# Sixteen-point stages of a 2-D spectral filter: sixteen bursts of one row, or eleven of three rows

## The chip, the cores and the metric

The kernel runs on one core of a Trainium2 chip. The metric is device time in microseconds of one execution. The engines are TensorE (PE, with its weight loads as PEld), VectorE (DVE), ScalarE (ACT), GpSimd (POOL) and SyncE (SP), which here issues the DMAs.

## The reference

```python
x = A_x                       # (1, 2048, 640), bf16
xn = layernorm(x)
X = rfft2(xn over (2048, 640))
s = irfft2(X * (w_r + 1j * w_i))          # 2048 x 321 complex filter
g = silu((gelu(xn @ w_gate) * (xn @ w_up)) @ w_down)   # 640 -> 1536 -> 640
return x + s * g
```

So there are two branches from the same normalised input: a spectral filter (a two-dimensional real transform, a product with a complex filter, the inverse transform) and a gated FFN. They meet in one product and one sum.

## The kernel before, in words

The 2048 rows are split as 16 x 128. The forward transform goes in three stages: a 128-point stage per slab (`slab_S1`), the transform along the 640 columns (`pair_D`), which gives 321 frequencies, and a stage of sixteen points across the slabs. The last needs the data in another order, so `pair_D` stores its result to a scratch array in device memory (`ZDR`) and `load_B2` brings it back as `B2`, 128 partitions by 32 rows by 321 frequencies. The inverse goes the same way back: a sixteen-point stage, a scratch array `UDR`, `load_V`, a 128-point stage (`slab_S1i`) and the inverse along the columns (`pair_Di`).

The change touches the sixteen-point stages. Before, there are sixteen bursts, one for each h from 0 to 15. `pair_S2(h)` makes four matmuls of 64 x 64 weights (the four quadrants of the array) over the 321 frequencies of rows h and 16+h of `B2` into a pair of PSUM banks `px`. ScalarE copies `px` to `xs` (642 elements a partition), VectorE multiplies it with the filter's real part (`W1`) and imaginary part (`W2`), giving two products. `pair_S2i(h)` makes eight more matmuls of the two products into another pair of banks `pu`, the first four from the first product, the last four from the second. ScalarE copies `pu` out in two instructions, even and odd frequencies, into `us`, and SyncE stores `us` to `UDR` in two DMAs. Row 0 needs a matrix of its own in one of the quadrants (`kind`). The two PSUM pairs come from one pool of two.

The order on every engine is written out by hand. A list `back` has 144 steps: pieces of the FFN, which are either a half (`ffn_half`: five matmuls of 512 columns) or a third of the down projection (`down_third`: eight matmuls of 320 columns). `plan` says what of the spectral branch is put behind each step. `load_B2` stands behind step 54. The bursts stand behind steps 64 to 88: `pair_S2(h)` behind step 64 + 3h//2, and `pair_S2i(h-1)` right after it; the last `pair_S2i` and `load_V` stand behind step 88. So two bursts are one or two steps apart by turns. Steps 60 to 71 and 96 to 107 are down projections, 72 to 95 FFN halves. The first slab of the inverse 128-point stage stands behind step 96, and the gather that prepares it (`gather`, L579) behind step 95.

The filter rows come in 32 DMAs over SyncE (`w_rows`), and GpSimd halves the first and the last frequency (`w_edge`). The normalised input `X` (16 slabs of 640) is last read as a matmul or fold operand ahead of step 54; its slabs 12 to 15 are still read by transposing DMAs (`slab_T`) placed behind steps 65, 68, 71 and 74.

Of the kernel before, what the change touches and what calls it, by code (L numbers as in the profile page):

```python
# [10 lines left out]
BF16 = mybir.dt.bfloat16  # L11
INT32 = mybir.dt.int32
ACT = mybir.ActivationFunctionType
ALU = mybir.AluOpType
P = 128
S = 2048
D = 640
L = 321
LP = 322
LH = 161  # L20
# [3 lines left out]
NS = 16  # L24
NH = 32
# [5 lines left out]
@with_exitstack  # L31
def kernel(
    ctx: ExitStack,
    tc: tile.TileContext,
    A_x: bass.AP,
    A_w_r: bass.AP,
    A_w_i: bass.AP,
    B_x: bass.AP,
    B_w_gate: bass.AP,
    B_w_up: bass.AP,  # L40
    B_w_down: bass.AP,
    out: bass.AP,
):

    nc = tc.nc
    x2 = A_x[0]
    xv = x2.rearrange("(n2 n1) d -> n2 n1 d", n1=NS)
    outv = out[0].rearrange("(n2 n1) d -> n1 n2 d", n1=NS)  # L50

    consts = ctx.enter_context(tc.tile_pool(name="consts", bufs=1))
    big = ctx.enter_context(tc.tile_pool(name="big", bufs=1))
    wts = ctx.enter_context(tc.tile_pool(name="wts", bufs=1))
    xg = ctx.enter_context(tc.tile_pool(name="xg", bufs=5))
    work = ctx.enter_context(tc.tile_pool(name="work", bufs=2))
    psA = ctx.enter_context(tc.tile_pool(name="psA", bufs=2, space=bass.MemoryType.PSUM))
    psB = ctx.enter_context(tc.tile_pool(name="psB", bufs=2, space=bass.MemoryType.PSUM))
    dram = ctx.enter_context(tc.tile_pool(name="dscratch", bufs=1, space=bass.MemoryType.DRAM))

    ZDR = dram.tile([2, NS, P, L], BF16)
    UDR = dram.tile([2, NS, P, L], BF16)


    X = big.tile([P, NS, D], BF16, tag="sX")
    Wg = wts.tile([P, 5, F], BF16)
    Wu = wts.tile([P, 5, F], BF16)
    Wd = wts.tile([P, NT, D], BF16)
    W1 = wts.tile([P, NS, 2, L], BF16)
    W2 = wts.tile([P, NS, 2, L], BF16)  # L70
    wgv = B_w_gate.rearrange("(c p) f -> p c f", p=P)
    wuv = B_w_up.rearrange("(c p) f -> p c f", p=P)
    with tc.manual_schedule():
        build(nc, locals())


def build(nc, env):
    consts, big, wts, xg, work, psA, psB = (env[k] for k in ("consts", "big", "wts", "xg", "work", "psA", "psB"))
    ZDR, UDR, X, Wg, Wu, Wd, W1, W2 = (env[k] for k in ("ZDR", "UDR", "X", "Wg", "Wu", "Wd", "W1", "W2"))
    xv, outv, wgv, wuv = (env[k] for k in ("xv", "outv", "wgv", "wuv"))  # L80
# [28 lines left out]

    spw = [(WT, src.rearrange("(k1 r) l -> k1 r l", k1=NS)) for WT, src in ((W1, A_w_r), (W2, A_w_i))]  # L110

    def w_rows(i, hh, ri, pm):
        WT, sp = spw[i]
        p0 = hh * 64 + ri * 2 + pm
        for lo in range(2):
            u0 = lo * 32 + hh * 16
            if pm == 0:
                nc.sync.dma_start(out=WT[p0:p0 + 61:4, :, lo, :], in_=sp[:, u0:u0 + 16, :])
            elif u0 == 0:
                nc.sync.dma_start(out=WT[p0:p0 + 61:4, 1:NS, lo, :], in_=sp[:, 127:112:-1, :])  # L120
                nc.sync.dma_start(out=WT[p0:p0 + 61:4, 0, lo, :], in_=sp[:, 64, :])
            else:
                nc.sync.dma_start(out=WT[p0:p0 + 61:4, :, lo, :], in_=sp[:, 128 - u0:112 - u0:-1, :])

    def w_edge(i):
        WT = spw[i][0]
# [7 lines left out]
    MG = consts.tile([P, 2, 2, 64], BF16)  # L134
    N1 = consts.tile([P, 2, P], BF16)
    N2 = consts.tile([P, 2, P], BF16)
# [29 lines left out]
    xf = {}  # L166
# [347 lines left out]
    st_b = {}  # L514

    def load_B2():
        B2 = big.tile([P, NH, L], BF16, tag="sB", name="B2")
        zv = ZDR.rearrange("c n (z a k h) l -> a (c n z) k h l", z=2, a=2, k=2)
        B4 = B2.rearrange("p (k h) l -> p k h l", k=2)
        for h0, h1 in ((0, 1), (1, 4), (4, 8), (8, 12), (12, 16)):  # L520
            for lo in range(2):
                nc.sync.dma_start(out=B4[64 * lo:64 * lo + 64, :, h0:h1, :], in_=zv[lo][:, :, h0:h1, :])
        st_b["B2"] = B2

    def pair_S2(h):
        B2 = st_b["B2"]
        px = psB.tile([P, 2, 512], FP32, tag="b")
        for lo in range(2):
            r = slice(64 * lo, 64 * lo + 64)
            for hh in range(2):  # L530
                kind = 0 if h == 0 and lo == 0 and hh == 0 else 1
                nc.tensor.matmul(px[64 * hh:64 * hh + 64, lo, 0:L], lhsT=MG[r, kind, 0, :], rhs=B2[r, 16 * hh + h, :],  # L532
                                 start=True, stop=True)
        xs = work.tile([P, 2 * L], BF16, tag="m1", bufs=2)
        nc.scalar.copy(out=xs.rearrange("p (k l) -> p k l", k=2), in_=px[:, :, 0:L])  # L535
        p1 = work.tile([P, 2 * L], BF16, tag="p1", bufs=2)
        p2 = work.tile([P, 2 * L], BF16, tag="p2", bufs=2)
        for pp, WT in ((p1, W1), (p2, W2)):
            nc.vector.tensor_tensor(out=pp, in0=xs, in1=WT[:, h].rearrange("p k l -> p (k l)"), op=ALU.mult)  # L539
        st_b[h] = (p1, p2)  # L540

    uv = UDR.rearrange("c n (z a h) l -> a (c n z) h l", z=2, a=2)

    def pair_S2i(h):
        p1, p2 = st_b.pop(h)
        pu = psB.tile([P, 2, 512], FP32, tag="b")
        for NM, pp, first in ((N1, p1, True), (N2, p2, False)):
            for hh in range(2):
                r = slice(64 * hh, 64 * hh + 64)
                for lo in range(2):  # L550
                    kind = 0 if h == 0 and lo == 0 and hh == 0 else 1
                    nc.tensor.matmul(pu[64 * lo:64 * lo + 64, hh, 0:L], lhsT=NM[r, kind, 0:64],  # L552
                                     rhs=pp[r, lo * L:(lo + 1) * L], start=first, stop=not first)
        us = work.tile([P, 2, L], BF16, tag=("xf", "uv")[h % 2], bufs=2, name="us")
        nc.scalar.copy(out=us[:, :, 0:LH], in_=pu[:, :, 0:L:2])
        nc.scalar.copy(out=us[:, :, LH:L], in_=pu[:, :, 1:L:2])
        for lo in range(2):
            nc.sync.dma_start(out=uv[lo][:, h:NH:16, :], in_=us[64 * lo:64 * lo + 64, :, :])

    st_c = {}  # L560

# [189 lines left out]
    def put(s, *item):  # L751
        plan[s].append(item)
# [57 lines left out]
    for pair in range(8):  # L810
        a = F0 + 3 * pair
# [3 lines left out]
        if pair < 6:  # L815
            b = a if pair < 4 else a + 3
# [6 lines left out]
    for k in range(16):  # L823
        put(8 + k if k < 8 else (32, 35, 38, 41, 44, 44, 47, 47)[k - 8], w_rows, k // 8, k % 8 // 4, k % 2, k % 4 // 2)
    put(40, w_edge, 0)
    put(z_end + 4, w_edge, 1)
    put(z_end, load_B2)
    put(z_end + 3, mg_turn)
    sb = z_end + 10
    for h in range(NS):  # L830
        put(sb + 3 * h // 2, pair_S2, h)
        if h > 0:
            put(sb + 3 * h // 2, pair_S2i, h - 1)
    sb += 24
    put(sb, pair_S2i, NS - 1)
    put(sb, load_V)
    vs0 = sb + 8
    for i, at in enumerate((vs0 - 1, vs0, vs0 + 6, vs0 + 16, vs0 + 25)):
# [2 lines left out]
    for pair in range(8):  # L841
        a = vs0 + 11 * pair // 2
# [55 lines left out]
```

## Time and profile before

| | |
|---|---|
| median of three runs | 207.86 us (207.09 to 207.91) |
| the profiled execution | 207.12 us |
| its span, first to last instruction | 205.3 us |
| granted TensorE clock, mean | 0.997 |
| TensorE busy | 198.7 us |
| ScalarE, VectorE, GpSimd busy | 124.7, 129.9, 33.9 us |

How to read it: a row of a timeline has the start, the length, the engine, the line of the kernel, the operation, what it writes and reads, the shape and how many instructions were merged; in brackets, how long the engine had been idle and whom it waited for. A matmul's length includes a modelled tail, so the distance between starts tells more. A row of a group (by line and shape) has the total busy time and the mean length of one in ns, then the idle time before them. A DMA row has the number of DMAs, the size of one, and the median time from issue to landing.

### The profile page before, as it was taken

The numbers are of one execution on the slowest core, as the hardware profiler recorded it, in microseconds if no ns is written. First come the engines' busy times: TensorE is split into PE (matmuls) and PEld (weight loads), VectorE is DVE, ScalarE is ACT, GpSimd is POOL, SyncE is SP. The second block draws the span as 40 slices with busy tenths as digits, with TensorE's granted clock in tenths as the row PEclk, the third lists the DMA queues.
The fourth block names the chain that finished last, engine by engine and source line by source line (L and its number), as shares of the span: only waits on it lengthen the run. The fifth ranks groups of instructions, "written<-read, shape, count | busy, mean of one in ns | idle before, by whom it ended". The sixth has DMA issues, their size and how long they took to land.

```text
span 205.3 us, 4412 instructions
## 1 busy us (share of the span) xinstructions
PE 198.7 (97%) x1626; PEld 121.2 (59%) x1643; DVE 129.9 (63%) x357; ACT 124.7 (61%) x230; POOL 33.9 (17%) x61
## 2 busy tenths in 40 slices
PE   7999999999999999999999999999999999999993
PEld 5788855777555555475644444447775555556762
DVE  7886966797678842336565655433568768775653
ACT  2547567767868787225787777424555654656641
POOL 5328688945001100000000000000000000000000
PEclk9999999999999999999999999999999999999998
DMA  5999999899987799289965332369731332242111
GB/s 168 303 305 314 369 291 135 168 146 179 176 161 169 166 186 172 68 198 229 192 137 108 73 67 65 82 139 294 228 86 74 96 123 74 63 132 78 66 51 65
DMA packets 46199, 31.81 MB, mean 155 GB/s; under 512 B 12512, under 2 KB 43872, under 8 KB 46176
## 3 DMA queue, kind: packets, MB, share of 16 engines
q1 hardware_dynamic: 46176, 31.52, 67.1%
q8 instruction: 13, 0.21, 0.5%
q14 instruction: 10, 0.08, 0.1%
HBM read 21.66 MB, written 7.88 MB: 144 GB/s over the span
## 4 chain that ended last, share of the span: by engine, by line
PE 90%; DVE 4%; DMA 2%; issue 1%; ACT 1%; POOL 1%; SPq 0%; DVEq 0%
PE psu L670 24%; PE psg L670 24%; PE psg L694 13%; PE psu L694 12%; PE pd L490 5%; PE pu L552 3%; PE pv L597 2%; PE pz L481 2%; DMA X<-in_A_x_dram 2%; PE pd L494 2%; PE px L532 2%; DVE st L174 1%; DVE uT L676 1%; POOL rst L190 1%; PE pt L326 0%
## 5 line engine op out<-in xcount | busy, mean ns | idle before, releaser
L670 PE MATMUL psu<-xnT,Wu 128*128 128x512 bf16 (+2 forms) x289 | 60.4, 339 | 0.6 <-issue 0.3
L670 PE MATMUL psg<-xnT,Wg 128*128 128x512 bf16 (+2 forms) x284 | 59.9, 338 | 0.8 <-issue 0.3
L676 DVE TENSOR_TENSOR uT<-psu,ge 128x512 bf16<-128x512 f32 (+2 forms) x59 | 34.4, 586 | 33.7 <-PE psu L670 27.4
L674 ACT ACTIVATE ge<-psg 128x512 bf16<-128x512 f32 (+2 forms) x59 | 30.6, 518 | 28.9 <-PE psg L670 27.6
L694 PEld LDWEIGHTS <-uT 128*128 128x128 bf16 x384 | 36.1, 98 | 15.2 <-issue 0.5
L670 PEld LDWEIGHTS <-Wu 128*128 128x128 bf16 x295 | 26.5, 98 | 21.8 <-issue 1.3
L670 PEld LDWEIGHTS <-Wg 128*128 128x128 bf16 x295 | 26.2, 98 | 20.9 <-issue 1.0
L694 PE MATMUL psg<-Wd,uT 128*128 128x320 bf16 (+1 forms) x192 | 30.4, 303 | 0.0
L694 PE MATMUL psu<-Wd,uT 128*128 128x320 bf16 (+1 forms) x192 | 29.6, 296 | 0.0
L539 DVE TENSOR_TENSOR p<-xs,W 128x642 bf16<-128x642 bf16 x32 | 14.4, 492 | 8.9 <-ACT xs L535 8.5
L502 ACT CAST zd<-pd 128x644 bf16<-128x644 f32 x15 | 12.3, 883 | 4.6 <-PE pd L494 4.6
L611 ACT ACTIVATE eo<-pd 128x640 bf16<-128x640 f32 x16 | 10.4, 701 | 7.4 <-PE pd L494 7.4
L599 ACT CAST vs<-pv 128x640 bf16<-128x640 f32 x16 | 11.0, 690 | 6.1 <-PE pv L597 6.1
L174 DVE BATCH_NORM_STATS2 st<-X 128x6 f32<-128x320 bf16 x32 | 14.1, 481 | 0.3 <-issue 0.2
L535 ACT CAST xs<-px 128x642 bf16<-128x642 f32 x16 | 11.1, 692 | 4.0 <-PE px L532 3.6
L620 DVE TENSOR_TENSOR cs<-eo 128x640 bf16<-128x640 bf16 x16 | 7.1, 485 | 7.5 <-ACT eo L611 7.5
L483 ACT CAST Z<-pz 128x640 bf16<-128x640 f32 x16 | 11.0, 694 | 1.1 <-PE pz L481 1.1
L190 POOL TENSOR_TENSOR rst<-ve,mhalf 128x1 f32<-128x1 f32 (+2 forms) x9 | 6.5, 719 | 27.2 <-DVE ve L188 27.2
L645 DVE TENSOR_TENSOR Yall<-Yall,G 128x640 bf16<-128x640 bf16 (+3 forms) x18 | 8.1, 450 | 1.8 <-ACT G L699 1.6
L703 DVE SCALAR_TENSOR_TENSOR G<-th,psg 128x320 bf16<-128x320 f32 x8 | 3.9, 486 | 7.6 <-ACT th L702 7.6
L646 DVE TENSOR_TENSOR Yall<-Yall,xt 128x640 bf16<-128x640 bf16 (+3 forms) x18 | 8.2, 454 | 0.6
L552 PE MATMUL pu<-p,N 64*64 64x321 bf16 x128 | 8.2, 304 | 0.1
(138 smaller groups left out, 213.1 us busy)
## 6 DMA issues: line engine op xcount, KB each, us to landing
ZDR<-zd SPq DMA_DIRECT2D x16, 160.5 KB, 4.2
UDR<-us SPq DMA_DIRECT2D x32, 80.2 KB, 2.6
xt<-in_A_x_dram SPq DMA_DIRECT2D x8, 320.0 KB, 3.2
W<-in_A_w_r_dram SPq DMA_DIRECT2D x14, 160.5 KB, 6.8
W<-in_A_w_i_dram SPq DMA_DIRECT2D x14, 160.5 KB, 5.1
out_dram<-Yall SPq DMA_DIRECT2D x14, 160.0 KB, 1.8
B<-ZDR SPq DMA_DIRECT2D x6, 321.0 KB, 8.4
Vin<-UDR SPq DMA_DIRECT2D x6, 321.0 KB, 5.8
```

What stands on the lines that cost most here:

```text
L174: nc.vector.bn_stats(out=st[:, k, :], in_=X[:, n1, 320 * k:320 * k + 320])
L483: nc.scalar.copy(out=Zt[n1], in_=pz)
L502: ev(out=zd.rearrange("p a c (m b) -> p a c m b", b=2)[:, :, :, :, b], in_=pd[b])
L535: nc.scalar.copy(out=xs.rearrange("p (k l) -> p k l", k=2), in_=px[:, :, 0:L])
L539: nc.vector.tensor_tensor(out=pp, in0=xs, in1=WT[:, h].rearrange("p k l -> p (k l)"), op=ALU.mult)
L552: nc.tensor.matmul(pu[64 * lo:64 * lo + 64, hh, 0:L], lhsT=NM[r, kind, 0:64], rhs=pp[r, lo * L:(lo + 1) * L], start=first, stop=not first)
L599: nc.scalar.copy(out=vs, in_=pv)
L611: nc.scalar.activation(out=eo[:, b], in_=py[b], func=ACT.Copy, scale=(2.0 if n0 // 4 in BY_SILU else 1.0) / (S * D))
L670: nc.tensor.matmul(ps, lhsT=WT[:, c, t * P:(t + 1) * P], rhs=xnT[g][:, c, c0:c1_], start=(c == 0), stop=(c == 4))
L674: nc.scalar.activation(out=ges[t], in_=ps, func=ACT.Gelu_apprx_tanh)
L676: nc.vector.tensor_tensor(out=uT[g][:, t, c0:c1_], in0=ps, in1=ges[t], op=ALU.mult)
L694: nc.tensor.matmul(ph, lhsT=uT[g][:, t, j * P:(j + 1) * P], rhs=Wd[:, t, c0:c1_], start=(t == 0), stop=(t == NT - 1))
```

## The change

A burst is now three rows h by about half of the frequencies: 162 or 159, so 486 or 477 columns of a PSUM bank. Rows 0 to 14 make ten such bursts, row 15 alone an eleventh of 321 columns. The matmuls, the copy to `xs`, the two products and the copies to `us` work on three rows at once. The frequencies of a row are split over two bursts, and both write into one `us` of three whole rows, which is stored in two DMAs once the second half is there. In the first two bursts, the quadrant that treats row 0 apart has two matmuls in place of one.

The filter tiles are laid out with rows of 322 elements and the two halves (`lo`) outside of the rows. The products and `us` no longer have tiles of their own: they lie in the first 13 slabs of `X`, two sets of each by turns. `load_B2` brings rows 0 to 2, 3 to 5, 6 to 8, 9 to 11 and 12 to 15, where it was 0, 1 to 3, 4 to 7, 8 to 11 and 12 to 15. Burst b stands behind step 64 + 24b//11, its second half behind the next burst's first, and the last second half behind step 87. `load_V` stays behind step 88.

```diff
-    W1 = wts.tile([P, NS, 2, L], BF16)
-    W2 = wts.tile([P, NS, 2, L], BF16)
+    W1 = wts.tile([P, 2, NS, LP], BF16)
+    W2 = wts.tile([P, 2, NS, LP], BF16)
...
-        for h0, h1 in ((0, 1), (1, 4), (4, 8), (8, 12), (12, 16)):
+        for h0, h1 in ((0, 3), (3, 6), (6, 9), (9, 12), (12, 16)):
...
+        sc = X[:, 0:13, :].rearrange("p n d -> p (n d)")
+        n_u, n_p = 2 * 3 * L, 2 * 3 * WB
+        st_b["p"] = sc[:, 0:4 * n_p].rearrange("p (s q k x) -> p s q k x", s=2, q=2, k=2)
+        st_b["u"] = sc[:, 4 * n_p:4 * n_p + 2 * n_u].rearrange("p (s k x) -> p s k x", s=2, k=2)
+
+    WB = LH + 1
+    BURSTS = [(h0, 3, l0, w) for h0 in range(0, 15, 3) for l0, w in ((0, WB), (WB, L - WB))]
+    BURSTS.append((15, 1, 0, L))
+
+    def s2_tiles(b, lo, hh):
+        h0, n = BURSTS[b][:2]
+        if h0 == 0 and lo == 0 and hh == 0:
+            return ((0, 1, 0), (1, n, 1))
+        return ((0, n, 1),)
...
-                kind = 0 if h == 0 and lo == 0 and hh == 0 else 1
-                nc.tensor.matmul(px[64 * hh:64 * hh + 64, lo, 0:L], lhsT=MG[r, kind, 0, :], rhs=B2[r, 16 * hh + h, :],
-                                 start=True, stop=True)
+                for i, j, kind in s2_tiles(b, lo, hh):
+                    ps = px[64 * hh:64 * hh + 64, lo, i * w:j * w].rearrange("p (h l) -> p h l", l=w)
+                    nc.tensor.matmul(ps, lhsT=MG[r, kind, 0, :],
+                                     rhs=B2[r, 16 * hh + h0 + i:16 * hh + h0 + j, l0:l0 + w], start=(i == 0),
+                                     stop=(j == n))
+
+        def wide(t):
+            return t[:, :, 0:n * (WB if n > 1 else LP)].rearrange("p k (h l) -> p k h l", h=n)[:, :, :, 0:w]
+
+        xs = wide(work.tile([P, 2, 3 * WB], BF16, tag="m1", bufs=2, name="xs"))
+        nc.scalar.copy(out=xs, in_=px[:, :, 0:n * w].rearrange("p k (h l) -> p k h l", l=w))
+        pp = []
+        for q, WT in enumerate((W1, W2)):
+            pp.append(wide(st_b["p"][:, b % 2, q]))
+            nc.vector.tensor_tensor(out=pp[-1], in0=xs, in1=WT[:, :, h0:h0 + n, l0:l0 + w], op=ALU.mult)
...
-        nc.scalar.copy(out=us[:, :, 0:LH], in_=pu[:, :, 0:L:2])
-        nc.scalar.copy(out=us[:, :, LH:L], in_=pu[:, :, 1:L:2])
-        for lo in range(2):
-            nc.sync.dma_start(out=uv[lo][:, h:NH:16, :], in_=us[64 * lo:64 * lo + 64, :, :])
+        us = st_b["u"][:, h0 // 3 % 2, :, 0:n * L].rearrange("p k (h l) -> p k h l", l=L)
+        pv = pu[:, :, 0:n * w].rearrange("p k (h l) -> p k h l", l=w)
+        for m in range(2):
+            c0 = m * LH + l0 // 2
+            nc.scalar.copy(out=us[:, :, :, c0:c0 + (w + 1 - m) // 2], in_=pv[:, :, :, m:w:2])
+        if l0 + w == L:
+            for lo in range(2):
+                nc.sync.dma_start(out=uv[lo][:, :, h0:h0 + n, :], in_=us[64 * lo:64 * lo + 64, :, :, :])
...
-    for h in range(NS):
-        put(sb + 3 * h // 2, pair_S2, h)
-        if h > 0:
-            put(sb + 3 * h // 2, pair_S2i, h - 1)
+    for b in range(len(BURSTS)):
+        put(sb + 24 * b // 11, s2_in, b)
+        if b > 0:
+            put(sb + 24 * b // 11, s2_out, b - 1)
+    put(sb + 23, s2_out, len(BURSTS) - 1)
     sb += 24
-    put(sb, pair_S2i, NS - 1)
     put(sb, load_V)
```

More of the change, by code (lines that the diff above doesn't have):

```diff
@@ L117, in w_rows @@
             if pm == 0:
-                nc.sync.dma_start(out=WT[p0:p0 + 61:4, :, lo, :], in_=sp[:, u0:u0 + 16, :])
+                nc.sync.dma_start(out=WT[p0:p0 + 61:4, lo, :, 0:L], in_=sp[:, u0:u0 + 16, :])
             elif u0 == 0:
-                nc.sync.dma_start(out=WT[p0:p0 + 61:4, 1:NS, lo, :], in_=sp[:, 127:112:-1, :])
-                nc.sync.dma_start(out=WT[p0:p0 + 61:4, 0, lo, :], in_=sp[:, 64, :])
+                nc.sync.dma_start(out=WT[p0:p0 + 61:4, lo, 1:NS, 0:L], in_=sp[:, 127:112:-1, :])
+                nc.sync.dma_start(out=WT[p0:p0 + 61:4, lo, 0, 0:L], in_=sp[:, 64, :])
             else:
-                nc.sync.dma_start(out=WT[p0:p0 + 61:4, :, lo, :], in_=sp[:, 128 - u0:112 - u0:-1, :])
+                nc.sync.dma_start(out=WT[p0:p0 + 61:4, lo, :, 0:L], in_=sp[:, 128 - u0:112 - u0:-1, :])
     def w_edge(i):
@@ L523, in load_B2, with s2_in @@
         st_b["B2"] = B2
-    def pair_S2(h):
+        sc = X[:, 0:13, :].rearrange("p n d -> p (n d)")
[10 more added lines that the diff above has]
+        return ((0, n, 1),)
+    def s2_in(b):
         B2 = st_b["B2"]
+        h0, n, l0, w = BURSTS[b]
         px = psB.tile([P, 2, 512], FP32, tag="b")
@@ L530, in pair_S2, with s2_out @@
             for hh in range(2):
-                kind = 0 if h == 0 and lo == 0 and hh == 0 else 1
-                nc.tensor.matmul(px[64 * hh:64 * hh + 64, lo, 0:L], lhsT=MG[r, kind, 0, :], rhs=B2[r, 16 * hh + h, :],
-                                 start=True, stop=True)
[L534 to L545, printed above, removed]
+                for i, j, kind in s2_tiles(b, lo, hh):
[11 more added lines that the diff above has]
+            nc.vector.tensor_tensor(out=pp[-1], in0=xs, in1=WT[:, :, h0:h0 + n, l0:l0 + w], op=ALU.mult)
+        st_b[b] = pp
+    uv = UDR.rearrange("c n (z a k h) l -> a (c n z) k h l", z=2, a=2, k=2)
+    def s2_out(b):
+        h0, n, l0, w = BURSTS[b]
+        pp = st_b.pop(b)
         pu = psB.tile([P, 2, 512], FP32, tag="b")
-        for NM, pp, first in ((N1, p1, True), (N2, p2, False)):
+        for q, NM in enumerate((N1, N2)):
             for hh in range(2):
@@ L550, in pair_S2i @@
                 for lo in range(2):
[L551 to L554, printed above, removed]
-        nc.scalar.copy(out=us[:, :, 0:LH], in_=pu[:, :, 0:L:2])
-        nc.scalar.copy(out=us[:, :, LH:L], in_=pu[:, :, 1:L:2])
-        for lo in range(2):
-            nc.sync.dma_start(out=uv[lo][:, h:NH:16, :], in_=us[64 * lo:64 * lo + 64, :, :])
+                    for i, j, kind in s2_tiles(b, lo, hh):
+                        ps = pu[64 * lo:64 * lo + 64, hh, i * w:j * w].rearrange("p (h l) -> p h l", l=w)
+                        nc.tensor.matmul(ps, lhsT=NM[r, kind, 0:64], rhs=pp[q][r, lo, i:j, :],
+                                         start=(q == 0 and i == 0), stop=(q == 1 and j == n))
+        us = st_b["u"][:, h0 // 3 % 2, :, 0:n * L].rearrange("p k (h l) -> p k h l", l=L)
[6 more added lines that the diff above has]
+                nc.sync.dma_start(out=uv[lo][:, :, h0:h0 + n, :], in_=us[64 * lo:64 * lo + 64, :, :, :])
     st_c = {}
```

## The prediction

> **What bounds the kernel now.** I read the page first: TensorE is busy for 97% of the span at full clock, and the chain that ended last is 90% TensorE.
>
> ```profile
> span 205.3 us, 4412 instructions
> PE 198.7 (97%) x1626; PEld 121.2 (59%) x1643; DVE 129.9 (63%) x357; ACT 124.7 (61%) x230; POOL 33.9 (17%) x61
> PEclk9999999999999999999999999999999999999998
> PE 90%; DVE 4%; DMA 2%; issue 1%; ACT 1%; POOL 1%; SPq 0%; DVEq 0%
> ```
>
> So an edit is worth what it takes from TensorE's own sequence, and nothing else, unless it makes TensorE wait. A busy figure hides small losses between matmuls, so I next read TensorE's timeline through the edited stage, 92 to 131 us, in order of starts.
>
> ```profile
> 91.86 0.71 PE L694 MATMUL psu<-Wd,uT 128*128 128x320 bf16 x4
> 92.50 0.33 PE L532 MATMUL px<-B,MG 64*64 64x321 bf16 x4
> 92.77 1.26 PE L694 MATMUL psu<-Wd,uT 128*128 128x320 bf16 x8
> ...
> 96.47 0.71 PE L694 MATMUL psu<-Wd,uT 128*128 128x320 bf16 x4
> 97.10 0.33 PE L532 MATMUL px<-B,MG 64*64 64x321 bf16 x4
> 97.26 0.45 PE L552 MATMUL pu<-p,N 64*64 64x321 bf16 x8
> 97.64 1.26 PE L694 MATMUL psu<-Wd,uT 128*128 128x320 bf16 x8
> ...
> 120.98 1.25 PE L670 MATMUL psu<-xnT,Wu 128*128 128x512 bf16 x5
> 122.16 0.33 PE L532 MATMUL px<-B,MG 64*64 64x321 bf16 x4
> 122.44 0.60 PE L552 MATMUL pu<-p,N 64*64 64x321 bf16 x8
> 122.98 1.25 PE L670 MATMUL psg<-xnT,Wg 128*128 128x512 bf16 x5
> ...
> 128.70 1.24 PE L670 MATMUL psg<-xnT,Wg 128*128 128x512 bf16 x5
> 129.87 0.47 PE L552 MATMUL pu<-p,N 64*64 64x321 bf16 x8
> 130.27 1.25 PE L670 MATMUL psu<-xnT,Wu 128*128 128x512 bf16 x5
> 131.36 1.24 PE L670 MATMUL psg<-xnT,Wg 128*128 128x512 bf16 x5
> 139.75 1.79 PE L694 MATMUL psu<-Wd,uT 128*128 128x320 bf16 x12
> 141.38 0.39 PE L597 MATMUL pv<-Tinv,Vin 128*128 128x128 bf16 x4
> ```
>
> A printed length includes a modelled tail; start-to-start is what counts. Five FFN matmuls of 512 columns take 131.36 - 130.27, about 1.08 us (0.216 each); twelve of 320 take 141.38 - 139.75 = 1.63 us (0.136 each). Both give about 0.42 ns a column. From the end of the down matmuls ahead of the first px (91.86 + 4 x 0.136 = 92.40) to the FFN piece after the last pu (130.27) are 37.87 us. Between lie steps 65 to 88: seven down thirds of eight matmuls (7 x 1.09) and seventeen FFN halves (17 x 1.08), 25.98 us. The sixteen-point stages cost TensorE **11.89 us**.
>
> Four 64*64 matmuls run side by side, so a burst streams three times 321 columns (one px round, two pu rounds): 3 x 0.136 = 0.41 us, and all sixteen 6.54 us. The other 5.35 us has two parts. One is a cost per group, a stretch of 64*64 work between two stretches of 128*128 work. The group at 97.10 takes 97.64 - (96.47 + 0.54) = 0.63 us for 0.41 of columns: 0.22 lost. The px alone at 92.50 loses 0.37 - 0.14 = 0.23, the pu alone at 129.87 0.49 - 0.27 = 0.22. There are 17 groups: 3.74 us. The rest, 1.61 us, is waiting. Group 122.16 takes 122.98 - (120.98 + 1.08) = 0.92 us, 0.29 more than a clean one; its px-to-pu distance is 0.28 against 0.16. It has one FFN step between itself and the group before, where 97.10 has two. With one step the products are not ready:
>
> ```profile
> 121.04 0.69 ACT L535 CAST xs<-px 128x642 bf16<-128x642 f32 x1
> 121.76 0.90 DVE L539 TENSOR_TENSOR p<-xs,W 128x642 bf16<-128x642 bf16 x2 [1.41 <-ACT xs L535]
> ```
>
> The second product ends at 122.66, after the pu that uses it has started. Half the steps of the old rhythm (3h//2) are such one-step gaps.
>
> **The change part by part.** TensorE: 16 bursts become 11 (five of 486 columns, five of 477, one of 321), so the columns are the same: 5 x 3 x (0.205 + 0.201) + 0.41 = 6.50 us. Groups fall from 17 to 12 (11 with a px, and the last pu alone): 12 x 0.22 = 2.64 us, a gain of 1.10. In the first two bursts one of the four quadrants is cut in two (row 0 has its own matrix); the other three quadrants start behind the 162-column piece, 0.07 us, at two px and two pu: at most 0.28 us, at least nothing. I take all of it.
>
> Waits: the new rhythm (24b//11) has no gap under two steps, but each burst's chain is longer. I follow it from the start of px, with these rows:
>
> ```profile
> 97.53 0.69 ACT L535 CAST xs<-px 128x642 bf16<-128x642 f32 x1 [0.43 <-PE px L532]
> 98.26 0.90 DVE L539 TENSOR_TENSOR p<-xs,W 128x642 bf16<-128x642 bf16 x2 [0.63 <-ACT xs L535]
> L539 DVE TENSOR_TENSOR p<-xs,W 128x642 bf16<-128x642 bf16 x32 | 14.4, 492 | 8.9 <-ACT xs L535 8.5
> L452 DVE TENSOR_TENSOR f<-uvt 128x512 bf16<-128x512 bf16 x16 | 6.8, 422 | 1.5 <-PE pz L481 1.3
> L453 DVE TENSOR_TENSOR f<-uvt 128x128 bf16<-128x128 bf16 x16 | 3.5, 218 | 0.0
> L629 DVE TENSOR_TENSOR Yall<-cs 128x640 bf16<-128x640 bf16 x8 | 3.9, 483 | 0.0
> L535 ACT CAST xs<-px 128x642 bf16<-128x642 f32 x16 | 11.1, 692 | 4.0 <-PE px L532 3.6 <-ACT us L556 0.4
> L556 ACT CAST us<-pu 128x320 bf16<-128x320 f32 x16 | 7.2, 451 | 0.0
> L676 DVE TENSOR_TENSOR uT<-psu,ge 128x512 bf16<-128x512 f32 x40 | 27.5, 688 | 31.1 <-PE psu L670 25.7 <-ACT ge L674 1.7 <-PE psg L670 1.5
> L676 DVE TENSOR_TENSOR uT<-psu,ge 128x256 bf16<-128x256 f32 x13 | 5.3, 412 | 2.5 <-PE psu L670 1.7 <-ACT ge L674 0.8
> ```
>
> Before, xs starts 0.43 us after px; with 486 columns 0.50. ACT's slope is (692 - 451)/322 = 0.75 ns an element, so xs of 972 takes 0.94 us, and the first product starts at 1.48. All-bf16 products have a slope of (422 - 218)/384 = 0.53 ns: 492 + 330 x 0.53 = 0.67 us each, with 0.41 + 0.18 = 0.59 from start to start (two take 0.90 now). The second ends at 1.48 + 0.59 + 0.67 = 2.74. The next px starts 0.84 (a burst) + 2.16 (two steps) = 3.0 after this one, its first pu round at 3.2 and the second, which reads the second product, at 3.4. Slack: 0.67 us; an activation ahead of xs, which delays it by 0.1 to 0.2, fits in. I take zero waits; the ends are nothing and the 1.61 us of now.
>
> This holds if rows cost nothing. A product now runs over rows of 162 or 159 at pitches of 162 and 322. L629 runs over reversed rows of 160 at 483 ns, as fast as anything flat, so for even rows I take the flat rate. No row of the trace has odd rows; the ends are the flat rate and that of L676 (one f32 input), (688 - 412)/256 = 1.08 ns an element or 1.18 us. L629 is nearest, so the flat rate. For a moving operand in three rows no row exists either: from nothing to 0.026 us a row edge (px to pu takes 0.16 for 0.136 of columns), and with two edges a round, 60 edges, 1.6 us. I take nothing, because px reads rows that start at odd elements every second time, all alike:
>
> ```profile
> L532 PE MATMUL px<-B,MG x64: 321/322/323, 92.5 to 127.0; 64*64 64x321 bf16 x64
> ```
>
> ACT: 48 copies become 33, elements the same; a burst's ACT work (xs 0.94, two us of about 0.57, one ge of 0.60, by their lengths) is 2.7 us in 3.0, less when start-to-start is counted (us copies follow each other by 0.32 us at a length of 0.44). It frees the PSUM pair in time, with some 0.7 us to spare. DVE: 32 products become 22, cover unchanged. POOL's filter edge has the same size. SP: 32 stores become 12, ten of three rows; the filter loads and the transposes are as many as before, two transposes now going ahead of the first store, which frees the others behind them. All that is off TensorE's path.
>
> Loads: the first B pair grows from one row to three.
>
> ```profile
> 85.93 7.32 SPq L522 DMA_DIRECT2D B<-ZDR  x10
> B<-ZDR SPq DMA_DIRECT2D x2, 80.2 KB, 2.6
> B<-ZDR SPq DMA_DIRECT2D x2, 240.8 KB, 4.9
> B<-ZDR SPq DMA_DIRECT2D x6, 321.0 KB, 8.4
> 134.78 6.58 SPq L569 DMA_DIRECT2D Vin<-UDR  x10
> 140.41 0.30 DVE L579 COPY vr<-Vin 128x128 bf16<-128x128 bf16 x2 [1.40 <-DMA Vin<-UDR]
> ```
>
> The same 240.8 KB behind another pair lands in 4.9 us, so at the head of the queue by about 87.2 + 4.9 = 92.1 at the latest, 0.4 before px needs it: nothing, and the margin is thin. The Vin load starts when the last store has landed; the last pu moves from step 88 to step 87, so Vin gains a step. Scratch for products and us lies in the dead slabs of X; its one overlap with a transpose still in flight (slab 12) is written seven steps after that is issued.
>
> **Sum.** 6.50 + 2.64 + 0.28 = 9.42 us against 11.89: 2.47 us gained, 1.10 from groups, 1.61 from waits, 0.04 from columns, less 0.28. The profiled execution took 207.12 us; the median of the runs is 207.86 and the mean of all four 207.50. From the mean I get 205.0 (204.65 from the profiled one).
>
> **Rivals.** [...] At 1.18 us each (1.10 start to start) the second ends at 1.48 + 1.10 + 1.18 = 3.76, its pu round stands at 3.4: 0.36 us of stall at nine bursts (not behind the three-step gap nor the last, short one), 3.2 us, less 2.47: 0.8 us slower, 208.3. It decides from about 1.06 us start to start. For it: both operands and the result now have row gaps. Against: L629 and L452.
>
> *Only odd rows fall.* The 159-wide products stall four times, 1.4 us: gain 1.0, 206.5. [...]
>
> *Row edges cost TensorE* 1.6 us: gain 0.9, 206.6.
>
> *The first B pair is late.* If it needs the 8.4 us of the big loads from 86.5, px starts at 94.9 instead of 92.5 and the gain is gone: 207.4.
>
> **How the numbers follow.** Forecast 0.64, its own range 204.0 (nothing for the cut quadrant, and a low run of 207.09 less 2.75, with 0.3 of scatter) to 205.8 (0.8 us of waits left). Odd rows or row edges, 206.5: 0.16. All products slow, 208.3: 0.12. B late, 207.4: 0.08. Up to 207.4 the cases hold about 0.85; without the late load, which the upper end takes in, it would be under 0.8. A measurement here tells 0.5%, 1.04 us, from no change: the forecast and about 0.10 of the second case are faster, 0.06 of it and 0.05 of the late load are the same, the rest slower.
>
> **What would show it.** Right: products of 0.66 us in both widths, xs of 0.94, groups of 0.84, px-to-pu distances of one round everywhere, 9.4 us of stage. Wrong: products over 1.0 us, or waits of pu for them; a px round well over 0.205; a first px later than 92.5; DVE waiting longer for Vin.

## The result, and the profile after

The changed kernel takes 204.68 us (median; 204.64 to 204.89) against 207.57 us (207.08 to 208.68) for the kernel before on the same chip: a ratio of 0.987, 95% interval 0.985 to 0.989. The profiled execution took 204.67 us with a span of 202.6, 2.45 us under the profiled execution of before. One execution on record, of the kernel with unpadded filter rows further down, took 1144.57 us at a granted clock of 1.0; the ratios leave it out, and its cause is not known.

TensorE's timeline of the changed kernel through the same stage (start, length, what, how many):

```profile
91.84 0.71 PE L720 MATMUL psu<-Wd,uT 128*128 128x320 bf16 x4
92.48 0.40 PE L548 MATMUL px<-B,MG 64*64 64x162 bf16 x5
92.81 1.26 PE L720 MATMUL psu<-Wd,uT 128*128 128x320 bf16 x8
93.91 1.25 PE L720 MATMUL psg<-Wd,uT 128*128 128x320 bf16 x8
95.09 0.40 PE L548 MATMUL px<-B,MG 64*64 64x159 bf16 x5
95.33 0.58 PE L575 MATMUL pu<-X,N 64*64 64x162 bf16 x10
95.83 0.72 PE L720 MATMUL psg<-Wd,uT 128*128 128x320 bf16 x4
...
113.05 1.24 PE L696 MATMUL psu<-xnT,Wu 128*128 128x512 bf16 x5
114.22 0.40 PE L548 MATMUL px<-B,MG 64*64 64x477 bf16 x4
114.45 0.58 PE L575 MATMUL pu<-X,N 64*64 64x486 bf16 x8
114.96 1.25 PE L696 MATMUL psg<-xnT,Wg 128*128 128x512 bf16 x5
...
126.56 1.25 PE L696 MATMUL psg<-xnT,Wg 128*128 128x512 bf16 x5
```

The stage is summed as before: from 91.84 + 4 x 0.136 = 92.38 to 126.56 are 34.18 us; between lie steps 65 to 87, seven down thirds and sixteen FFN halves, 24.90 us. The sixteen-point stages now cost TensorE **9.28 us**, 2.61 less than the 11.89 of before. The two spans differ by 2.7 us (205.3 and 202.6), so the stage is nearly all of that, and no later stage gave anything back. The times differ by only 2.45: what an execution takes outside its span is 1.8 us in the kernel before (mean of 24 executions) and 2.0 to 2.1 in the six of the changed kernel. No run here shows why.

Two things are to be seen in the rows. Each group takes its columns and a fixed rest: the one at 114.22 takes 114.96 - (113.05 + 1.08) = 0.83 us for 3 x 0.20 of columns. And px to pu is one round in every group: 0.23 to 0.24 us in the bursts of three rows, 0.16 in the last one of 321 columns. There is no group like that at 122.16 in the kernel before.

The group rows, by shape, of the products and of ScalarE's copies, in the changed kernel:

```profile
L560 DVE TENSOR_TENSOR X<-xs,W 128x972 bf16<-128x972 bf16 x10 | 6.2, 662 | 3.8 <-ACT xs L556 2.8 <-DMA B<-ZDR 0.9
L560 DVE TENSOR_TENSOR X<-xs,W 128x954 bf16<-128x954 bf16 x10 | 6.2, 660 | 4.2 <-ACT xs L556 4.2
L556 ACT CAST xs<-px 128x972 bf16<-128x972 f32 x5 | 4.8, 967 | 1.8 <-PE px L548 1.8
L581 ACT CAST X<-pu 128x486 bf16<-128x486 f32 x10 | 5.7, 573 | 0.2
```

The products in rows of 159 cost the same as those in rows of 162, and both stay at the flat rate of the forecast (0.67 us for 972 elements).

### The profile page after: what moved, and what is told of

It reads as the page before. It is cut to its first block, busy times and chain, and to the rows that moved or that the text cites. A ratio compares the mean times of both kernels' runs of the same rounds, so it can differ in the third digit from the quotient of the medians.

```text
span 202.6 us, 4240 instructions
## 1 busy us (share of the span) xinstructions
PE 196.3 (97%) x1572; PEld 119.7 (59%) x1589; DVE 129.0 (64%) x347; ACT 124.3 (61%) x215; POOL 33.9 (17%) x61
## 4 chain that ended last, share of the span: by engine, by line
PE 91%; DVE 4%; DMA 1%; issue 1%; POOL 1%; ACT 0%; DVEq 0%
PE psu L696 24%; PE psg L696 24%; PE psg L720 13%; PE psu L720 12%; PE pd L490 5%; PE pv L623 2%; PE pu L575 2%; PE pz L481 2%; PE pd L494 2%; PE px L548 2%; DVE st L174 2%; DMA X<-in_A_x_dram 1%; POOL rst L190 1%; DVE X L196 1%; DVE uT L702 1%
## 5 line engine op out<-in xcount | busy, mean ns | idle before, releaser
L560 DVE TENSOR_TENSOR X<-xs,W 128x972 bf16<-128x972 bf16 (+2 forms) x22 | 13.3, 646 | 8.2 <-ACT xs L556 7.3
L556 ACT CAST xs<-px 128x972 bf16<-128x972 f32 (+2 forms) x11 | 10.3, 938 | 4.6 <-PE px L548 4.6
L581 ACT CAST X<-pu 128x486 bf16<-128x486 f32 (+4 forms) x22 | 12.2, 556 | 1.2 <-PE pu L575 0.8
```

Of the source, the lines that this page charges most:

```text
L556: nc.scalar.copy(out=xs, in_=px[:, :, 0:n * w].rearrange("p k (h l) -> p k h l", l=w))
L560: nc.vector.tensor_tensor(out=pp[-1], in0=xs, in1=WT[:, :, h0:h0 + n, l0:l0 + w], op=ALU.mult)
L581: nc.scalar.copy(out=us[:, :, :, c0:c0 + (w + 1 - m) // 2], in_=pv[:, :, :, m:w:2])
```

## The experiments

All are compared with a kernel before that ran on the same chip: 207.15 us for the first four, 207.10 for the next two, 207.28 for the last two.

### The old bursts with the products used one burst later

```diff
-        put(sb + 3 * h // 2, pair_S2, h)
-        if h > 0:
-            put(sb + 3 * h // 2, pair_S2i, h - 1)
+        if h > 1:
+            put(sb + 3 * h // 2, pair_S2i, h - 2)
+        put(sb + 3 * h // 2, pair_S2, h)
+    put(sb + 23, pair_S2i, NS - 2)
```

> The kernel before with one edit: a burst's products are used one burst later, so that no product can be late, and there are 18 groups of 64*64 work where there were 17. Theory (a price of 0.22 us per group, and 1.6 us of waiting for products): the waits go, one group is added, 207.57 - 1.6 + 0.22 = 206.2 us, and every group has a px-to-pu distance of one round. Rival (the one-step groups are long for a reason of their own, the gain of the change came from larger bursts alone): no faster than 207.5, and the groups after one step still take 0.74 us and more.

Measured: 205.87 us, ratio 0.993 (0.991 to 0.995). TensorE's timeline of this kernel, a group after two steps and one after one step, and the ends of the stage:

```profile
91.77 0.71 PE L694 MATMUL psu<-Wd,uT 128*128 128x320 bf16 x4
...
119.05 0.47 PE L552 MATMUL pu<-p,N 64*64 64x321 bf16 x8
119.35 0.31 PE L532 MATMUL px<-B,MG 64*64 64x321 bf16 x4
119.59 1.25 PE L670 MATMUL psu<-xnT,Wu 128*128 128x512 bf16 x5
120.78 0.47 PE L552 MATMUL pu<-p,N 64*64 64x321 bf16 x8
121.07 0.31 PE L532 MATMUL px<-B,MG 64*64 64x321 bf16 x4
121.32 1.25 PE L670 MATMUL psg<-xnT,Wg 128*128 128x512 bf16 x5
...
129.01 1.25 PE L670 MATMUL psu<-xnT,Wu 128*128 128x512 bf16 x5
```

Both groups take 0.54 us from the first pu to the next FFN matmul. The stage costs 129.01 - 92.31 - 25.98 = 10.72 us, which is 6.54 of columns and 18 groups of 0.23. So the waits of the kernel before were waits on what the last group had left to do (a product, or a PSUM pair to be copied out; more on that below), and can be had back without any larger burst: with one group more, the stage is 1.17 us shorter, of the 2.61 of the change. The rival, that a group after one step is long for a reason of its own, falls.

### The changed kernel with twice as many groups

```diff
-            put(sb + 24 * b // 11, s2_out, b - 1)
+            put(sb + 24 * b // 11 + 1, s2_out, b - 1)
```

> The changed kernel with a burst's second half one step behind the next burst's first half, so that the same matmuls stand in 22 groups where there were 12. Theory (0.22 us per group): 204.68 + 10 x 0.22 = 206.9 us. Rival (the fixed cost belongs to the matmuls or their rounds, not to the change between 64*64 and 128*128 work): 204.7 us.

Measured: 207.01 us, 2.33 over the changed kernel, for ten groups more: **0.23 us a group**. A stretch of its timeline:

```profile
112.61 1.25 PE L696 MATMUL psg<-xnT,Wg 128*128 128x512 bf16 x5
113.79 0.60 PE L575 MATMUL pu<-X,N 64*64 64x477 bf16 x8
114.32 1.25 PE L696 MATMUL psu<-xnT,Wu 128*128 128x512 bf16 x5
115.50 0.40 PE L548 MATMUL px<-B,MG 64*64 64x477 bf16 x4
115.84 1.25 PE L696 MATMUL psg<-xnT,Wg 128*128 128x512 bf16 x5
```

The same pu takes 114.32 - (112.61 + 1.08) = 0.63 for 0.40 of columns, the px 115.84 - (114.32 + 1.08) = 0.44 for 0.20. The price hangs on the change between 64*64 and 128*128 work, whatever stands in the group, and not on the number of matmuls, which is the same. A change of work alone does not cost it: in the kernel before, five 128*128 matmuls of the inverse 128-point stage stand between two pieces of the down projection, from 141.38 on.

```profile
141.60 0.22 PE L597 MATMUL pv<-Tinv,vr 128*128 128x128 bf16 x1
141.66 1.52 PE L694 MATMUL psg<-Wd,uT 128*128 128x320 bf16 x10
```

The twelve matmuls ahead of them started at 139.75 and take 1.63 us, so nothing is lost on the way in, and 141.66 - 141.38 = 0.28 us is 0.27 for five times 128 columns at 0.42 ns, with 0.01 left.

### The changed kernel with bursts one step apart

```diff
-        put(sb + 24 * b // 11, s2_in, b)
+        put(sb + 16 * b // 11, s2_in, b)
         if b > 0:
-            put(sb + 24 * b // 11, s2_out, b - 1)
-    put(sb + 23, s2_out, len(BURSTS) - 1)
+            put(sb + 16 * b // 11, s2_out, b - 1)
+    put(sb + 16, s2_out, len(BURSTS) - 1)
```

> The changed kernel with its bursts behind step 64 + 16b//11, so that six of ten gaps are one step, as half of them were in the kernel before; the last second half moves with them, the Vin load stays where it is. Theory (the two-step gaps hide the products, by some 0.7 us): a one-step gap brings the next second pu round to 2.33 us after px, the second product ends at 2.7: 0.4 us of wait at six bursts, 2.4 us, 207.1 us. Rival (no waits were in play, the number of bursts decides): 204.7 us.

Measured: 207.24 us, 2.56 over the changed kernel; ratio to before 1.000 (0.998 to 1.002). With the same eleven bursts and twelve groups the whole gain is gone. The size was as expected, the reason only in part. TensorE, ScalarE and VectorE around a group after one step, in this kernel:

```profile
105.70 1.25 PE L696 MATMUL psg<-xnT,Wg 128*128 128x512 bf16 x5
106.89 0.40 PE L548 MATMUL px<-B,MG 64*64 64x486 bf16 x4
107.49 0.60 PE L575 MATMUL pu<-X,N 64*64 64x477 bf16 x8 [0.20 <-ACT X L581]
108.02 1.25 PE L696 MATMUL psu<-xnT,Wu 128*128 128x512 bf16 x5
```

```profile
106.26 1.18 ACT L581 CAST X<-pu 128x486 bf16<-128x486 f32 x2
```

```profile
106.40 1.23 DVE L560 TENSOR_TENSOR X<-xs,W 128x954 bf16<-128x954 bf16 x2 [0.38 <-ACT xs L556]
```

The group takes 108.02 - (105.70 + 1.08) = 1.24 us, 0.41 more than a clean one. Its first pu starts at 107.49, just after ScalarE has finished copying out the pu of the burst before (106.26 + 1.18 = 107.44): it waited for the PSUM pair. The first product was there since about 107.06 (106.40 and the 0.66 us of one), and the second at 107.63, when the second round had not begun. So here it is ScalarE's two copies, and only in the first burst a product, that set the wait.

### The changed kernel with every product made twice

```diff
-            nc.vector.tensor_tensor(out=pp[-1], in0=xs, in1=WT[:, :, h0:h0 + n, l0:l0 + w], op=ALU.mult)
+            for _ in range(2):
+                nc.vector.tensor_tensor(out=pp[-1], in0=xs, in1=WT[:, :, h0:h0 + n, l0:l0 + w], op=ALU.mult)
```

> [...] Theory: the second product then ends at 1.44 + 3 x 0.58 + 0.66 = 3.84 us after px, the pu round that reads it stands at 3.44: 0.4 us of stall at nine bursts, 3.6 us, 208.3 us, slower than the kernel before. Rival (VectorE is far enough from TensorE's path that its pace is of no account): 204.7 to 205.2 us.

Measured: 209.02 us, ratio to before 1.007 (1.005 to 1.009): slower, by 4.3 us over the changed kernel where 3.6 were expected. TensorE of this kernel, two bursts, and then VectorE:

```profile
108.87 0.40 PE L548 MATMUL px<-B,MG 64*64 64x477 bf16 x4
109.10 0.38 PE L576 MATMUL pu<-X,N 64*64 64x486 bf16 x4
110.16 0.40 PE L576 MATMUL pu<-X,N 64*64 64x486 bf16 x4 [0.69 <-DVE X L561]
110.49 1.25 PE L697 MATMUL psu<-xnT,Wu 128*128 128x512 bf16 x5
...
113.83 0.40 PE L548 MATMUL px<-B,MG 64*64 64x486 bf16 x4
114.07 0.57 PE L576 MATMUL pu<-X,N 64*64 64x477 bf16 x8
```

```profile
107.47 2.64 DVE L561 TENSOR_TENSOR X<-xs,W 128x972 bf16<-128x972 bf16 x4 [0.86 <-ACT xs L556]
110.02 0.69 DVE L703 TENSOR_TENSOR uT<-psu,ge 128x512 bf16<-128x512 f32 x1
110.62 2.62 DVE L561 TENSOR_TENSOR X<-xs,W 128x954 bf16<-128x954 bf16 x4
```

Four products take 2.61 to 2.64 us, where two take 1.23 to 1.24 in the changed kernel, and where the rival with all products at 1.18 us has 1.10 + 1.18 = 2.28 for two. The second pu round waits for the second product, as expected, but not in every burst: the stalls are long (from 99 us on TensorE is idle for 0.42 to 0.69 us in the four bursts that have such a row) and come in every second one. In these four the second round starts 2.9 us later in all than a round of columns would have it, and the px at 99.12 is already 1.0 us later than the one at 98.11 in the changed kernel: 3.9 us, most of the 4.3. After a long stall or a three-step gap the next product is in time, or up to 0.2 us late. VectorE has no idle time between the four products, the FFN's uT and the next four, so a late burst also delays what is queued behind it. In the stretch 92 to 129 us it was busy for 32.5 of 37 us; in the changed kernel, 92 to 127, for 21.4 of 35. This is what the rival with all products at 1.18 us would have looked like.

### Filter rows without padding

```diff
-    W1 = wts.tile([P, 2, NS, LP], BF16)
-    W2 = wts.tile([P, 2, NS, LP], BF16)
+    W1 = wts.tile([P, 2, NS, L], BF16)
+    W2 = wts.tile([P, 2, NS, L], BF16)
```

> The changed kernel with filter rows of 321 elements in place of 322, so that every second row of the filter begins at an odd element, and nothing else. [...]

Measured: 204.77 us, ratio to before 0.988 (0.986 to 0.990). The question is whether products keep their 0.66 us when filter rows start at odd elements, or fall to the 1.18 us worked out from L676 of the kernel before. The product rows of this kernel:

```profile
L560 DVE TENSOR_TENSOR X<-xs,W 128x972 bf16<-128x972 bf16 x10 | 6.2, 665 | 3.8 <-ACT xs L556 2.8 <-DMA B<-ZDR 0.9
L560 DVE TENSOR_TENSOR X<-xs,W 128x954 bf16<-128x954 bf16 x10 | 6.2, 661 | 4.2 <-ACT xs L556 4.2
```

The products are as fast as with padding (665 and 661 ns here, 662 and 660 in the changed kernel): the padding is worth nothing here. Only the filter, one of the two inputs, has rows at odd starts in this run; `xs` and the result keep even ones. Rows of odd length cost nothing that shows either: 954 elements are six rows of 159, and take 661 ns where the slope of 0.53 ns an element, taken on flat rows, gives 492 + 312 x 0.53 = 657.

### Stores of one row at a time

```diff
-                nc.sync.dma_start(out=uv[lo][:, :, h0:h0 + n, :], in_=us[64 * lo:64 * lo + 64, :, :, :])
+                for i in range(n):
+                    nc.sync.dma_start(out=uv[lo][:, :, h0 + i:h0 + i + 1, :], in_=us[64 * lo:64 * lo + 64, :, i:i + 1, :])
```

> The changed kernel with each store of three rows cut into three stores of one row, 32 stores as in the kernel before. Theory (the stores are off TensorE's path, and the Vin load has a step of margin): 204.7 us, at most 0.3 us more if the Vin load becomes late for the first gather. Rival (the three-row stores are a part of the gain, by SyncE's time or the DMA queues): 205.5 us or more.

Measured: 204.70 us, ratio to before 0.988 (0.986 to 0.989): the larger stores are no part of the gain. The start of the Vin loads on SyncE's queue, first in the changed kernel, then with one-row stores:

```profile
130.55 6.43 SPq L595 DMA_DIRECT2D Vin<-UDR  x10
```

```profile
132.19 6.67 SPq L596 DMA_DIRECT2D Vin<-UDR  x10
```

The loads start 1.6 us later. VectorE then waits 1.2 us for one of them ahead of a gather, where it waited for none in the changed kernel, and TensorE does not notice: 204.70 us, where the changed kernel takes 204.68. That this margin comes from the last burst's earlier step was not tested.

### One group less

```diff
-    for b in range(len(BURSTS)):
-        put(sb + 24 * b // 11, s2_in, b)
-        if b > 0:
-            put(sb + 24 * b // 11, s2_out, b - 1)
-    put(sb + 23, s2_out, len(BURSTS) - 1)
+    put(sb, s2_in, 0)
+    put(sb, s2_in, 1)
+    for g in range(1, 10):
+        put(sb + 23 * g // 10, s2_out, g - 1)
+        put(sb + 23 * g // 10, s2_in, g + 1)
+    put(sb + 23, s2_out, 9)
+    put(sb + 23, s2_out, 10)
```

> The changed kernel with the first two px together behind step 64, then each pu of a burst ahead of the px two bursts later, and the last two pu together behind step 87: 11 groups of 64*64 work where there are 12, the same matmuls, products used a whole group later. Theory (0.23 us per group, nothing else left to gain): 0.23 us under the changed kernel, some 204.45 us. Rival (waits that the trace does not show are still in the stage): more than 0.5 us under it. If the PSUM pairs, now filled in the other order, make TensorE wait: over it.

> The changed kernel once more, beside the kernel with one group less on the same chip: 204.7 us.

Measured: 204.52 us (204.32 to 205.27) with eleven groups, 204.74 (204.50 to 204.87) with twelve; ratios to before 0.9866 and 0.9869, with intervals of 0.002 on either side. The totals differ by what was expected, but by no more than their runs scatter. The stage itself shows it, in TensorE's timeline with eleven groups:

```profile
91.93 0.71 PE L720 MATMUL psu<-Wd,uT 128*128 128x320 bf16 x4
92.56 0.61 PE L548 MATMUL px<-B,MG 64*64 64x162 bf16 x10
...
126.41 1.25 PE L696 MATMUL psg<-xnT,Wg 128*128 128x512 bf16 x5
```

126.41 - 92.47 - 24.90 = 9.04 us, 0.24 under the 9.28 of twelve groups. What is left of the stage is columns and groups (6.50 + 11 x 0.23 = 9.03), and nothing hidden beside them.

## Why the prediction was right, point by point

The prediction held in direction, size and for the most part in mechanism: 2.47 us of gain forecast for the stage, 2.61 measured there. That the two are so close is in part luck: the sum took 0.17 us too much for the waits of before and 0.28 for the cut quadrants, and these errors work against each other.

- *Price and number of groups.* Read as 0.22 us from single groups, measured as 0.23 over ten added ones. Five groups less: 1.15 us (forecast 1.10).
- *Waits.* With 0.23 a group, the kernel before waited 11.89 - 6.54 - 17 x 0.23 = 1.44 us (forecast 1.61), and the changed one 9.28 - 6.50 - 12 x 0.23 = 0.02. As long as products are used in the next group, it is the two-step rhythm that removes the waits, and the larger burst only makes room for it: older products remove them in the old bursts, and a rhythm of one and two steps brings back 2.6 us in the new ones.
- *The cut quadrant* was mis-sized: up to 0.28 us was taken, none is there. The group at 95.09, with ten pu matmuls in place of eight, takes 95.83 - (93.91 + 1.09) = 0.83 us like the others. Without this term the sum would have been 9.14.
- *The cause of the waits* was named too narrowly. "With one step the products are not ready" leaves out the PSUM pair. In the kernel before, the pu at 122.44 in the quoted group starts when ScalarE's second copy of the pu before it ends:

```profile
121.94 0.46 ACT L556 CAST us<-pu 128x320 bf16<-128x320 f32 x1
```

  and its second round, due at 122.44 + 0.14 = 122.58, then waits for the product that ends at 122.66. Both were at work in this group; using products a burst later removes both at once, so no run here parts them. The price, read from the distances, did not depend on it.
- *Rates.* Products 0.66 us in both widths (0.67 forecast), xs 0.97 us (0.94). In the changed kernel the second product of the px at 101.13 ends at 103.80, 2.67 after it (2.74 forecast; two of 1.23 us in all from 102.57). The slack was real but not large: with every product made twice the kernel is slower than before (209.02 us against 207.15). The rival with all products at 1.18 us had the right place and sign; its price was 0.8 us over before, the doubled products gave 1.9. The missed part is the queue behind the products.
- *Odd rows, row edges, a late first B pair.* None came. Odd rows cost nothing that shows, also without padding (660 and 661 ns for 954 elements). A px round of three rows takes 0.23 us to pu for 0.20 of columns, the same 0.03 over as a flat row had, so edges cost nothing that shows. The first px starts at 92.48, where it was 92.50. Its two loads are issued at 85.9 and 86.6 in the changed kernel's trace and land 3.7 and 4.1 us later, by 90.7: the margin is 1.8 us, where the forecast had 0.4.
- *The base.* The forecast was 205.0 because it stood on the mean of four executions, 207.50. From the profiled execution alone, 204.65, it would have been within 0.03 us of the median, but by luck: the span lost more than the forecast 2.47 us (2.7), and the 0.25 us or so that the changed kernel takes more outside its span, a term that the sum does not have, gave that back. The kernel before scatters upward, to 208.68, the changed one hardly.

## What to carry to other kernels

On an engine that is full, cost a stage by distances between starts: subtract the columns of the matmuls, and look at whether the rest goes with the number of changes between kinds of work, or with what each stretch waits for. Here one burst shape bought both at once, but about half of the gain was a matter of order alone, and the same shape in a tighter order lost all of it. Whoever lengthens a burst has to lengthen the distance between bursts, and to check each link of the chain (product, PSUM pair, queue behind the slow engine) against it.

## What had not been expected

- The cut matmul cost nothing with three others beside it: the five-matmul px at 92.48 takes 92.81 - 92.38 = 0.43 us, and 0.20 of columns with 0.23 for the group is the same.
- Rows of 159 elements, with every second filter row at an odd start, ran through VectorE at the flat rate of its bf16 products (661 ns for 954 elements; the slope of flat rows gives 657).
- VectorE at 88% of a stretch (32.5 of 37 us, every product made twice) already set TensorE's pace, with a stall of 0.42 us or more in every second burst.
